# Reciprocals spread two slots later, transposes next to the masks, pair 1 split earlier, first weights converted step by step

## The chip, the cores and the metric

The kernel runs on one core of a Trainium2 chip. The time is in device microseconds for one execution, and less is better. Five engines work beside each other, each on its own queue in order: TensorE (PE in the profile, with PEld for its weight loads), VectorE (DVE), ScalarE (ACT), GpSimd (POOL) and SyncE (SP), which issues the transfers. Semaphores join the queues.

## The reference

Causal attention over 2 x 12 heads with 448 tokens of 64 channels, then two dense blocks on the 896 x 768 result:

```python
scores = q @ k.T / 8, masked above the diagonal; attn = exp(scores - max) / (sum + 1e-9)
x = attn @ v                                        # heads side by side: 896 x 768
x = (sigmoid(x @ w_gate) * (x @ w_val)) @ w_out     # 768 -> 1536 -> 768
h = x @ w_in; s = h * softmax(h)                    # 768 -> 1024
out = layer_norm(s) * g_ln @ w_out2                 # 1024 -> 768
```

## The kernel before

Every float32 operand is split into a high and a low part, and a product is three matmuls of parts. The attention takes the 24 heads as 12 pairs. The dense stages follow (lines L574, L604, L634, L695); there TensorE runs without a break.

The order of the attention is written out by hand. A loop counts slots `s`; a pair `p` owns the slots from `8 p` on, so that eight slots are one period. The table `STEPS` holds (offset, engine, step): a step of pair `p` is issued in slot `8 p + offset`. In a slot each engine goes through the table once, in the table's order, and takes the steps that are due; each engine's queue then keeps that order. What the slots of a steady period hold, with the names used below:

- Scores: `sc_mm(p, g)` puts the mask into a PSUM tile by matmuls with an identity (L329), then adds q k (L338). Group 0 holds the query blocks with 448 and 64 keys, group 1 those with 320 and 192.
- Maxima: `sc_max` on VectorE (L351), one instruction for both heads of a pair: max-448 in slot 0, max-64 in slot 1, max-320 in slot 4, max-192 in slot 5.
- Exponentials: `sc_exp` on ScalarE (L358), two instructions (one per head) for each maximum, one or so slots later: exp-448, exp-64, exp-320, exp-192. Each also leaves its row sum in `sum_t`, the tile that the maxima are written to as well. VectorE therefore waits for exp-448 before max-64, and for exp-320 before max-192.
- Sums and reciprocals: `sums` on GpSimd (L363) after exp-192, `recips` on VectorE (L367) in the next pair's slot 0, ahead of that pair's max-448. `rs_wide` (L221, rx) spreads the reciprocals on GpSimd, `rs_mm` (L381, r) transposes them on TensorE, `rs_out` (L219, rb) copies them out on ScalarE.
- Transposes of the exponentials: `tr_mm` (L409, t) on TensorE four times a pair, each followed by `tr_hi` on ScalarE (L416, pt) and `tr_lo` on VectorE (L229, pt).
- Values: `pv_mm` (L441, x) in eight pieces, then `x_mul` on VectorE (L447, xf), `x_hi` on ScalarE (L219, xy) and `x_lo` on GpSimd (L229, xy), some 21 to 23 slots after the pair's first slot.
- Operands of the next pair: `prep_k_hi`, `prep_q_hi` on GpSimd, `prep_k_lo` (L229, qks) and `prep_q_lo` (L249, qks) on VectorE. The values are split on GpSimd (`prep_v_hi`, `prep_v_lo`: L229, v).
- Weights of the first dense stage: `bits_steps` converts a chunk in four steps, one on ScalarE (L112) and three on VectorE (L115, L117, L120); `chunk_hi` (ScalarE, L131) and `chunk_lo` (VectorE, L134) split it. Chunks 0 to 3 are converted from slot 88 on. From slot 96 on two of 36 matmuls of the first dense tile (L473, gv) are issued in each slot.
- `keep_warm(24)` in slots 2, 5 and 9 are matmuls that nobody reads (L308).

Of the kernel before, what the change touches and what calls it, by code (L numbers as in the profile page):

```python
# [12 lines left out]
BF16 = mybir.dt.bfloat16  # L13
# [31 lines left out]
def attn_moe_moe2(ctx: ExitStack, tc: tile.TileContext, qk, v, w_gv, w_out, w_in2, w_out2, g_ln, out):  # L45
# [3 lines left out]
    nc = tc.nc  # L49
# [9 lines left out]
    ident = const.tile([128, 128], F32, name="ident")  # L59
    identx = const.tile([128, 128], F32, name="identx")  # L60
    identb = const.tile([128, 128], BF16, name="identb")
    maskb = const.tile([128, 128], BF16, name="maskb")
    g_sb = const.tile([128, NF2], F32, name="g_sb")
    mhalf = const.tile([128, 1], F32, name="mhalf")

# [124 lines left out]
    with ExitStack() as actx:  # L190
# [80 lines left out]
        for i in range(2):  # L271
# [47 lines left out]
        def sc_mm(p, g):  # L319
            both = ps_s.tile([128, 2, 512], F32, tag="s", name="s")  # L320
            t = qk_sp[p]
            flat = t.rearrange("p c s -> p (c s)")
            c0 = 0
            for i in GROUPS[g]:
                n = QE[i]
                w = min(n, 128)
                ps = ps_sc[p, i] = both[:, :, c0:c0 + n]
                for e in range(2):
                    nc.tensor.matmul(out=ps[:, e, n - w:], lhsT=identb, rhs=maskb[:, 128 - w:],  # L329
                                     start=(c0 == 0), stop=False, skip_group_check=True)  # L330
                c0 += n
# [170 lines left out]

        def steps(s, eng):
            for s0, e, f in STEPS:
                p, r = divmod(s - s0, PER)
                if e == eng and r == 0 and (1 if s0 < 0 else 0) <= p < NPR:
                    f(p)


        for s in range(PER * NPR + 26):  # L510
            if s in (2, 5, 9):
                keep_warm(24)
# [10 lines left out]
            for c in range(2 * NE + 2):
                e = s - 88 - 9 * c
                if e == 0:
                    bits_now = bits_steps(c)
                if e in (0, 2, 4, 6):
                    next(bits_now)
                if e == 7 and c < 2 * NE:
                    chunk_hi(c)  # L530
                if e == 8 and c < 2 * NE:
                    chunk_lo(c)
# [230 lines left out]
```

## Time and profile before

| what | value |
|---|---|
| median of 3 runs | 514.15 us (514.12 to 514.21) |
| the profiled execution | 514.3 us, of which the span from the first to the last instruction is 512.5 us |
| granted TensorE clock, mean | 0.997 |
| attention with the first pairs' start | 0 to about 112 us |
| mixed end of attention and first dense tile | 110.8 to 129.5 us |
| dense stages | 129.5 to 512.5 us |

The span is the time between the first and the last instruction that the profiler saw; 1.8 us of the execution lie around it. A period of the attention is read from one max-448 to the next. A row of the timeline gives start, duration, engine, line, operation and operands; in brackets stands how long the engine sat idle before it and what released it. A wait for several semaphores is put down to the one that came last by the profile, so a name in brackets can be wrong where that engine had long been done.

### The profile page before, as it was taken

The numbers are of one execution on the slowest core, as the hardware profiler recorded it, in microseconds if no ns is written. First come the engines' busy times: TensorE is split into PE (matmuls) and PEld (weight loads), VectorE is DVE, ScalarE is ACT, GpSimd is POOL, SyncE is SP. The second block draws the span as 40 slices with busy tenths as digits, with TensorE's granted clock in tenths as the row PEclk, the third lists the DMA queues.
The fourth block names the chain that finished last, engine by engine and source line by source line (L and its number), as shares of the span: only waits on it lengthen the run. The fifth ranks groups of instructions, "written<-read, shape, count | busy, mean of one in ns | idle before, by whom it ended". The sixth has DMA issues, their size and how long they took to land.

```text
span 512.5 us, 7699 instructions
## 1 busy us (share of the span) xinstructions
PE 501.2 (98%) x2980; PEld 457.1 (89%) x2980; DVE 335.9 (66%) x512; ACT 226.4 (44%) x481; POOL 118.0 (23%) x203
## 2 busy tenths in 40 slices
PE   8899999989999999999999999999999999999997
PEld 8888888878899999999999999999998888899997
DVE  4578787887655777887777766766753887841210
ACT  4677777784532454345434432343324242432211
POOL 3375757552000000000000000000050587710000
PEclk9899999999999999999999999999999999999999
DMA  5632323112333154355433532354440221000101
GB/s 150 184 92 77 92 79 93 42 49 76 125 123 99 66 165 164 125 163 161 137 116 125 182 123 68 139 165 164 133 176 1 86 100 62 0 32 33 61 32 61
DMA packets 13204, 52.79 MB, mean 103 GB/s; under 512 B 1776, under 2 KB 2288, under 8 KB 13168
## 3 DMA queue, kind: packets, MB, share of 16 engines
q1 hardware_dynamic: 13168, 52.31, 31.4%
q8 instruction: 23, 0.38, 0.3%
q14 instruction: 13, 0.11, 0.1%
HBM read 49.55 MB, written 2.75 MB: 102 GB/s over the span
## 4 chain that ended last, share of the span: by engine, by line
PE 81%; DVE 6%; ACT 6%; POOL 5%; issue 1%; POOLq 0%; ACTq 0%
PE gv L574 33%; PE pm L604 17%; PE po L695 12%; PE h L634 11%; ACT p L358 4%; DVE sum L351 4%; POOL v L229 2%; DVE qks L229 2%; PE gv L473 1%; PE warm L308 1%; POOL rx L221 1%; PE tp L677 1%; PE x L441 1%; PE s L338 1%; PE t L409 1%
## 5 line engine op out<-in xcount | busy, mean ns | idle before, releaser
L574 PE MATMUL gv<-xy,hl 128*128 128x448 f32 x828 | 168.1, 365 | 0.6 <-ACT pre L478 0.6
L574 PEld LDWEIGHTS gv<-xy,hl 128*128 128x128 f32 x828 | 155.5, 188 | 13.2 <-ACT pre L478 1.0
L604 PE MATMUL pm<-g,hl 128*128 128x448 f32 x432 | 87.7, 365 | 0.0
L604 PEld LDWEIGHTS pm<-g,hl 128*128 128x128 f32 x432 | 81.2, 188 | 6.4
L621 POOL TENSOR_SCALAR t<-t,g_sb 128x768 f32<-128x768 f32 x8 | 9.0, 1123 | 248.1 <-PE pm L604 248.1
L134 DVE TENSOR_TENSOR hl<-t,hl 128x768 fp32r<-128x768 f32 x36 | 35.1, 975 | 40.2 <-ACT hl L131 38.4
L695 PE MATMUL po<-wo,lt 128*128 128x384 f32 x336 | 60.7, 340 | 0.0
L634 PE MATMUL h<-wi,xy 128*128 128x512 f32 x252 | 59.2, 395 | 0.0
L695 PEld LDWEIGHTS po<-wo,lt 128*128 128x128 f32 x336 | 58.7, 188 | 0.2 <-POOL wo L626 0.2
L358 ACT ACTIVATE p<-s,sum 128x448 f32<-128x448 f32 (+3 forms) x96 | 45.0, 478 | 29.9 <-DVE sum L351 14.9
L634 PEld LDWEIGHTS h<-wi,xy 128*128 128x128 f32 x252 | 47.2, 188 | 11.4
L120 DVE SCALAR_TENSOR_TENSOR t<-raw,t 128x768 int32<-128x768 int32 (+1 forms) x56 | 53.0, 946 | 1.7
L117 DVE SCALAR_TENSOR_TENSOR t<-raw,t 128x768 int32<-128x768 int32 (+1 forms) x56 | 52.6, 939 | 1.8
L441 PE MATMUL x<-pt,v 128*128 128x320 f32 (+3 forms) x252 | 53.5, 327 | 0.0
L112 ACT ACTIVATE raw<-raw 128x768 f32<-128x768 f32 (+1 forms) x56 | 47.9, 866 | 10.3 <-DMA raw<-in_wo_dram 6.0
L351 DVE TENSOR_REDUCE sum<-s 128x2 f32<-128x128 f32 (+3 forms) x47 | 31.6, 672 | 15.2 <-ACT p L358 13.4
L441 PEld LDWEIGHTS x<-pt,v 128*128 128x128 f32 x252 | 38.1, 190 | 2.0
L229 DVE TENSOR_TENSOR pt<-t,pt 128x512 fp32r<-128x512 f32 (+1 forms) x48 | 31.9, 667 | 3.8 <-ACT pt L416 3.8
L115 DVE TENSOR_SCALAR t<-raw 128x768 int32<-128x768 int32 (+1 forms) x56 | 30.6, 547 | 4.9 <-ACT raw L112 4.9
L171 DVE TENSOR_TENSOR lt<-tp,lt 128x512 fp32r<-128x512 f32 x14 | 9.7, 690 | 36.4 <-ACT lt L170 36.4
L131 ACT CAST hl<-t 128x768 fp32r<-128x768 f32 x36 | 30.0, 832 | 4.6 <-PE pm L604 4.2
L179 ACT ACTIVATE wk<-gv 128x448 f32<-128x448 f32 x23 | 11.3, 542 | 43.1 <-PE gv L574 43.1
(90 smaller groups left out, 542.7 us busy)
## 6 DMA issues: line engine op xcount, KB each, us to landing
raw<-in_gv_dram SPq DMA_DIRECT2D x24, 768.0 KB, 4.4
raw<-in_wo_dram SPq DMA_DIRECT2D x20, 768.0 KB, 4.3
raw<-in_wi_dram SPq DMA_DIRECT2D x12, 512.0 KB, 3.5
qkr<-in_qk_dram SPq DMA_DIRECT2D x22, 224.0 KB, 3.5
vr<-in_v_dram SPq DMA_DIRECT2D x12, 256.0 KB, 2.6
out_dram<-o SPq DMA_DIRECT2D x6, 384.0 KB, 2.3
qkr<-in_qk_dram SPq DMA_DIRECT2D x4, 112.0 KB, 2.7
out_dram<-o SPq DMA_DIRECT2D x2, 192.0 KB, 1.8
```

The source lines that it names most:

```text
L112: nc.scalar.activation(out=w1.bitcast(F32), in_=w1.bitcast(F32), func=AF.Copy, scale=2.0 ** -112)
L117: nc.vector.scalar_tensor_tensor(out=tt, in0=w1, scalar=-2 ** 31, in1=tt, op0=ALU.bitwise_and, op1=ALU.bitwise_or)
L120: nc.vector.scalar_tensor_tensor(out=tt, in0=w0, scalar=29, in1=tt, op0=ALU.logical_shift_right, op1=ALU.bitwise_or)
L134: nc.vector.tensor_tensor(out=lo, in0=t_t.pop(it), in1=f32(hi), op=ALU.subtract)
L229: (nc.gpsimd if eng == 'P' else nc.vector).tensor_tensor(out=out, in0=a, in1=b, op=ALU.subtract)
L351: nc.vector.reduce_max(out=sum_t[p % 3][:, 8 + i:16:NQ], in_=ps, axis=AX.X, negate=True)
L358: nc.scalar.activation(out=p_t[(2 * p + e) % NPB][:, POFF[i]:POFF[i] + n], in_=ps[:, 1 - e], func=AF.Exp, bias=mx, scale=1.0, accum_out=sm)
L441: nc.tensor.matmul(out=ps[:, 128 * j:], lhsT=l, rhs=pt_t[h][:, c, u, c0:c0 + S - 128 * j], start=(chunk == 0 and n == 0), stop=(chunk == 7 ...
L574: nc.tensor.matmul(out=ps[i, b], lhsT=w[:, a, cs], rhs=xy[kk][:, x, b * S:(b + 1) * S], start=(kk == 0 and a == 0 and x == 0), stop=(kk == ...
L604: nc.tensor.matmul(out=ps[b], lhsT=w[:, a, cs], rhs=g_t[kk][:, x, b * S:(b + 1) * S], start=(kk == 0 and a == 0 and x == 0), stop=(kk == N ...
L634: nc.tensor.matmul(out=h[:, n * 512:(n + 1) * 512], lhsT=xy[kk][:, a, tk], rhs=wi[n * NK + kk][:, c], start=(kk == 0 and i == 0), stop=(kk ...
L695: nc.tensor.matmul(out=ps[n], lhsT=lts[k // 4][:, a, k % 4], rhs=wo[k][:, c, cs], start=(k == 0 and i == 0), stop=(k == NF2 - 1 and i == 2))
```

## The change

The spreading of the reciprocals is issued two slots later (`rs_mm` offset 10 to 12, `rs_out` 11 to 13). The transposes move one slot and stand ahead of the scores in the table, so that two of a pair's four groups come directly in front of the mask matmuls. The pieces of `pv_mm` move by one slot. The mask of 448 and 64 keys becomes one matmul of 192 columns for each head in place of two. `x_mul` moves to the end of the table, behind the maxima. Pair 1's operands are split in slots 0 and 1, ahead of the maxima there. The last `keep_warm` has 12 matmuls. Chunks 0 and 1 of the weights are converted with one step in each of the periods from slot 18 on; chunk 2 follows in slots 102 to 114, and chunk 3 in the dense stage.

```diff
-    maskb = const.tile([128, 128], BF16, name="maskb")
+    maskb = const.tile([128, 192], BF16, name="maskb")
-        nc.vector.tensor_copy(out=maskb, in_=mask0)
+        nc.vector.tensor_copy(out=maskb[:, :128], in_=mask0)
+        nc.vector.tensor_copy(out=maskb[:, 128:], in_=mask0[:, 64:])
...
+            for n, (lo, hi) in enumerate(((320, 512),) if g == 0 else ((192, 320), (384, 512))):
                 for e in range(2):
+                    nc.tensor.matmul(out=both[:, e, lo:hi], lhsT=identb, rhs=maskb[:, :hi - lo], ...)
...
-              for u, a, s0 in ((1, 0, 9), (1, 1, 11), (0, 0, 13), (0, 1, 15))
-              for d, eng, f in ((0, 'E', tr_mm), (1, 'A', tr_hi), (2, 'D', tr_lo))),
-            *((13 + n, 'E', lambda p, n=n: pv_mm(p, n)) for n in range(len(CHUNKS))),
+              for u, a, s0 in ((1, 0, 10), (1, 1, 12), (0, 0, 14), (0, 1, 16))
+              for d, eng, f in ((0, 'E', tr_mm), (0, 'A', tr_hi), (1, 'D', tr_lo))),
+            *((14 + n, 'E', lambda p, n=n: pv_mm(p, n)) for n in range(len(CHUNKS))),
...
+        for c in range(2 * NE):
+            it = bits_steps(c)
+            for k in range(4):
+                weights[PER * (2 + 4 * c + k) + 2] = lambda it=it: next(it)
+            weights[PER * (2 + 4 * c + 3) + 3] = lambda c=c: chunk_hi(c)
+            weights[PER * (2 + 4 * c + 3) + 6] = lambda c=c: chunk_lo(c)
...
+            if s == 1:
+                prep_k_lo(1)
+                prep_q_lo(1)
```

VectorE, one steady period of before, from max-320 to the next pair's max-448 (`sum` is a maximum, `pt` a low part of a transpose, `xf` is `x_mul`, `qks` the operands, `rs` the reciprocals):

```order
L351 TENSOR_REDUCE sum_143<-s 128x2
L229 TENSOR_TENSOR pt<-t,pt 128x512
L447 TENSOR_TENSOR xf<-x,rb 128x448
L351 TENSOR_REDUCE sum_143<-s 128x2
L249 SCALAR_TENSOR_TENSOR qks<-qkr,qks 128x448
L229 TENSOR_TENSOR pt<-t,pt 128x448
L367 RECIPROCAL rs<-rs 128x8
L351 TENSOR_REDUCE sum_144<-s 128x2
```

The same place in the change, from a conversion step behind max-64 (L117) on:

```order
L117 SCALAR_TENSOR_TENSOR t<-raw,t 128x768
L229 TENSOR_TENSOR pt<-t,pt 128x512
L229 TENSOR_TENSOR qks<-qkr,qks 128x448
L352 TENSOR_REDUCE sum_144<-s 128x2
L229 TENSOR_TENSOR pt<-t,pt 128x512
L352 TENSOR_REDUCE sum_144<-s 128x2
L448 TENSOR_TENSOR xf<-x,rb 128x448
L249 SCALAR_TENSOR_TENSOR qks<-qkr,qks 128x448
L229 TENSOR_TENSOR pt<-t,pt 128x448
L368 RECIPROCAL rs<-rs 128x8
L352 TENSOR_REDUCE sum_145<-s 128x2
```

`x_mul` stood in front of max-192 and now stands behind it, and a conversion step has come between max-64 and the low part that follows.

ScalarE, the same place, before and then in the change (`rb` is `rs_out`, `xy` is `x_hi`; 320 and 192 are the exponentials):

```order
L219 COPY rb<-r 128x448
L416 CAST pt<-t 128x512
L358 ACTIVATE p_147,sum_142<-s,sum_142 128x320
L358 ACTIVATE p_148,sum_142<-s,sum_142 128x320
L416 CAST pt<-t 128x448
L219 CAST xy_76<-xf 128x448
L358 ACTIVATE p_147,sum_142<-s,sum_142 128x192
L358 ACTIVATE p_148,sum_142<-s,sum_142 128x192
```

```order
L417 CAST pt<-t 128x512
L219 COPY rb<-r 128x448
L359 ACTIVATE p_148,sum_143<-s,sum_143 128x320
L359 ACTIVATE p_149,sum_143<-s,sum_143 128x320
L417 CAST pt<-t 128x448
L219 CAST xy_76<-xf 128x448
L359 ACTIVATE p_148,sum_143<-s,sum_143 128x192
L359 ACTIVATE p_149,sum_143<-s,sum_143 128x192
```

`rs_out` moved behind a transpose's high part; `x_hi` stands, as before, in front of exp-192.

TensorE, around the second mask of a period, before and then in the change (`r` is `rs_mm`, `x` the values, `t` a transpose):

```order
L441 MATMUL x<-pt,v_0_138 128x448 x3
L381 MATMUL r<-identx,rx 128x128
L381 MATMUL r<-ident,rx 128x128 x3
L409 MATMUL t<-identx,p_148 128x128
L409 MATMUL t<-ident,p_148 128x128 x4
L441 MATMUL x<-pt,v_0_138 128x448 x2
L329 LDWEIGHTS identb
```

```order
L442 MATMUL x<-pt,v_1_140 128x448 x3
L410 MATMUL t<-identx,p_147 128x128
L410 MATMUL t<-ident,p_147 128x128 x4
L382 MATMUL r<-identx,rx 128x128
L382 MATMUL r<-ident,rx 128x128 x3
L331 LDWEIGHTS identb
```

`rs_mm` moved behind the transpose group, and the two matmuls of the values that stood between that group and the mask now come after the scores; the mask follows `rs_mm` directly.

## Rows read from the trace of the kernel before

**Rows 1.** page, part 1: busy time and share of the span, by engine
```profile
PE 501.2 (98%) x2980; PEld 457.1 (89%) x2980; DVE 335.9 (66%) x512; ACT 226.4 (44%) x481; POOL 118.0 (23%) x203
```

**Rows 2.** windows: stretch, us, busy (instructions) of PE, PEld, DVE, ACT, POOL, clock, DMA
```profile
57.94:66.68 8.74, 8.59 (x78) 7.58 (x78) 7.20 (x13) 6.64 (x24) 5.69 (x10) 1.00 0.31 83
...
101.57:110.76 9.19, 8.46 (x76) 7.32 (x75) 7.40 (x14) 7.45 (x24) 4.61 (x8) 1.00 0.00 1
110.76:129.50 18.74, 16.26 (x98) 14.20 (x96) 15.34 (x19) 9.95 (x20) 6.77 (x8) 1.00 0.25 85
129.50:297.60 168.10, 168.09 (x829) 155.86 (x830) 121.50 (x169) 71.15 (x109) 0.00 (x0) 1.00 0.41 136
```

**Rows 3.** timeline, one period, PE weight loads: start us, us, operands [idle before <-releaser]
```profile
61.42 0.14 PEld L381 LDWEIGHTS r<-identx,rx 128*128 128x128 f32 x1 [0.53 <-POOL rx L221]
```

**Rows 4.** timeline, the same period, VectorE
```profile
59.71 1.04 DVE L351 TENSOR_REDUCE sum<-s 128x2 f32<-128x896 f32 x1
...
62.22 0.29 DVE L351 TENSOR_REDUCE sum<-s 128x2 f32<-128x128 f32 x1 [0.87 <-ACT p L358]
...
62.70 0.69 DVE L229 TENSOR_TENSOR pt<-t,pt 128x512 fp32r<-128x512 f32 x1 [0.18 <-ACT pt L416]
...
65.60 0.61 DVE L447 TENSOR_TENSOR xf<-x,rb 128x448 f32<-128x448 f32 x1
...
66.28 0.56 DVE L351 TENSOR_REDUCE sum<-s 128x2 f32<-128x384 f32 x1
...
66.76 0.62 DVE L249 SCALAR_TENSOR_TENSOR qks<-qkr,qks 128x448 fp32r<-128x448 f32 x1
...
68.33 0.20 DVE L367 RECIPROCAL rs<-rs 128x8 f32<-128x8 f32 x1 [0.42 <-POOL rs L363]
```

**Rows 5.** timeline, the same period, ScalarE
```profile
65.12 0.53 ACT L358 ACTIVATE p<-s,sum 128x320 f32<-128x320 f32 x1 [0.95 <-DVE sum L351]
...
66.05 0.20 ACT L358 ACTIVATION_READ_ACCUMULATOR p<-s,sum 128x1 f32 x1
...
66.14 0.53 ACT L416 CAST pt<-t 128x448 fp32r<-128x448 f32 x1
...
66.56 0.58 ACT L219 CAST xy<-xf 128x448 fp32r<-128x448 f32 x1
...
67.02 0.44 ACT L358 ACTIVATE p<-s,sum 128x192 f32<-128x192 f32 x1
```

**Rows 6.** timeline, the same period, GpSimd
```profile
61.86 1.42 POOL L229 TENSOR_TENSOR v<-vr,v 128x384 fp32r<-128x384 f32 x2
...
68.04 0.26 POOL L363 TENSOR_SCALAR rs<-sum 128x8 f32<-128x8 f32 x1 [2.80 <-ACT p L358]
```

**Rows 7.** timeline, weight conversion on VectorE and a GpSimd subtract, end of the attention
```profile
106.06 0.75 DVE L115 TENSOR_SCALAR t<-raw 128x768 int32<-128x768 int32 x1
...
108.65 0.95 DVE L117 SCALAR_TENSOR_TENSOR t<-raw,t 128x768 int32<-128x768 int32 x1
...
119.97 1.14 POOL L229 TENSOR_TENSOR xy<-xf,xy 128x448 fp32r<-128x448 f32 x1 [3.27 <-ACT xy L219]
120.00 1.93 DVE L120 SCALAR_TENSOR_TENSOR t<-raw,t 128x768 int32<-128x768 int32 x1
```

**Rows 8.** timeline, the first three pairs, VectorE and PE
```profile
10.78 0.61 DVE L229 TENSOR_TENSOR qks<-qkr,qks 128x448 fp32r<-128x448 f32 x1
...
14.47 0.61 PEld L338 LDWEIGHTS s<-qks 64*128 64x128 f32 x8 [2.11 <-DVE qks L249]
...
15.33 1.04 DVE L351 TENSOR_REDUCE sum<-s 128x2 f32<-128x896 f32 x1
...
25.05 1.06 DVE L351 TENSOR_REDUCE sum<-s 128x2 f32<-128x896 f32 x1
```

**Rows 9.** timeline, after the last pair's exponentials, PE weight loads
```profile
112.71 0.14 PEld L409 LDWEIGHTS t<-identx,p 128*128 128x128 f32 x1 [1.04 <-ACT p L358]
...
115.04 0.14 PEld L381 LDWEIGHTS r<-identx,rx 128*128 128x128 f32 x1 [0.93 <-POOL rx L221]
```

More of the change, by code (lines that the diff above doesn't have):

```diff
@@ L324, in sc_mm @@
             for i in GROUPS[g]:
-                n = QE[i]
-                w = min(n, 128)
-                ps = ps_sc[p, i] = both[:, :, c0:c0 + n]
+                ps_sc[p, i] = both[:, :, c0:c0 + QE[i]]
+                c0 += QE[i]
+            for n, (lo, hi) in enumerate(((320, 512),) if g == 0 else ((192, 320), (384, 512))):
                 for e in range(2):
-                    nc.tensor.matmul(out=ps[:, e, n - w:], lhsT=identb, rhs=maskb[:, 128 - w:],
-                                     start=(c0 == 0), stop=False, skip_group_check=True)
-                c0 += n
+                    nc.tensor.matmul(out=both[:, e, lo:hi], lhsT=identb, rhs=maskb[:, :hi - lo],
+                                     start=(n == 0), stop=False, skip_group_check=True)
             for i in GROUPS[g]:
@@ L486, in attn_moe_moe2 @@
         STEPS = (
+            *((s0 + d, eng, lambda p, f=f, u=u, a=a: f(2 * p + a, u))
+              for u, a, s0 in ((1, 0, 10), (1, 1, 12), (0, 0, 14), (0, 1, 16))
+              for d, eng, f in ((0, 'E', tr_mm), (0, 'A', tr_hi), (1, 'D', tr_lo))),
+            (12, 'E', rs_mm),
             (0, 'E', lambda p: sc_mm(p, 0)), (4, 'E', lambda p: sc_mm(p, 1)),
-            *((s0 + d, eng, lambda p, f=f, u=u, a=a: f(2 * p + a, u))
-              for u, a, s0 in ((1, 0, 9), (1, 1, 11), (0, 0, 13), (0, 1, 15))
-              for d, eng, f in ((0, 'E', tr_mm), (1, 'A', tr_hi), (2, 'D', tr_lo))),
-            *((13 + n, 'E', lambda p, n=n: pv_mm(p, n)) for n in range(len(CHUNKS))),
-            (10, 'E', rs_mm),
+            *((14 + n, 'E', lambda p, n=n: pv_mm(p, n)) for n in range(len(CHUNKS))),
             (-7, ENG['kh'], prep_k_hi), (-6, ENG['qh'], prep_q_hi), (-5, ENG['kl'], prep_k_lo), (-2, 'D', prep_q_lo),
             (3, ENG['lk'], last_keys), (7, ENG['vh'], prep_v_hi), (9, ENG['vl'], prep_v_lo),
-            (7, 'P', sums), (8, 'D', recips), (8, ENG['rx'], rs_wide), (11, ENG['rr'], rs_out),
-            (21, 'D', x_mul), (22, ENG['xh'], x_hi), (23, ENG['xl'], x_lo),
+            (7, 'P', sums), (8, 'D', recips), (8, ENG['rx'], rs_wide), (13, ENG['rr'], rs_out),
+            (22, ENG['xh'], x_hi), (23, ENG['xl'], x_lo),
             (1, 'A', lambda p: sc_exp(p, 3)), (2, 'A', lambda p: sc_exp(p, 0)),
@@ L500, in attn_moe_moe2 @@
             (4, 'D', lambda p: sc_max(p, 2)), (5, 'D', lambda p: sc_max(p, 1)),
+            (21, 'D', x_mul),
         )
+        weights = {}
+        for c in range(2 * NE):
[4 more added lines that the diff above has]
+            weights[PER * (2 + 4 * c + 3) + 6] = lambda c=c: chunk_lo(c)
+        two = bits_steps(2 * NE)
+        for k in range(4):
+            weights[PER * NPR + 6 + 4 * k] = lambda: next(two)
         def steps(s, eng):
@@ L505, in steps @@
                 p, r = divmod(s - s0, PER)
-                if e == eng and r == 0 and (1 if s0 < 0 else 0) <= p < NPR:
+                if e == eng and r == 0 and (2 if s0 < 0 else 0) <= p < NPR:
                     f(p)
@@ L511, in attn_moe_moe2 @@
             if s in (2, 5, 9):
-                keep_warm(24)
+                keep_warm(24 if s < 9 else 12)
             steps(s, 'E')
@@ L517, in attn_moe_moe2 @@
             steps(s, 'A')
+            if s == 1:
+                prep_k_lo(1)
+                prep_q_lo(1)
             steps(s, 'D')
             steps(s, 'P')
+            if s == 0:
+                prep_k_hi(1)
+                prep_q_hi(1)
             if s in (8, 12):
                 dma_next()
[L523 to L532, printed above, removed]
+            if s in weights:
+                weights[s]()
         while left:
```

## Prediction

> **What bounds the kernel now.** The page's busy times come first [rows 1]. TensorE is busy for 98% of the span, and a reader might stop there. The windows by stage say more [rows 2]. From 129.50 us on TensorE works without a gap (168.09 of 168.10 us), so a microsecond that the attention loses or gains moves the end by a microsecond. In a steady attention period TensorE shows 8.59 of 8.74 us, but matmuls overlap in that figure; its weight loads fill 7.58 us. The timeline of one period then shows that TensorE even waits 0.53 us for the spread reciprocals [rows 3].
>
> What sets the 8.74 us is a ring through VectorE, ScalarE and GpSimd. To be seen in the timeline: max-448 starts at 59.71; max-64 waits 0.87 us for exp-448 and starts at 62.22; a transpose's low part (pt) follows at 62.70 after 0.18 us for its high part; behind it on VectorE stand the key's low part and max-320 [rows 4]. Exp-320 waits 0.95 us for that maximum and starts at 65.12; its second sum is read by 66.25; pt, `x_hi` (66.56) and exp-192 (67.02) follow without a gap [rows 5]. `sums` waits for exp-192 and starts at 68.04 [rows 6], the reciprocals wait for `sums` (68.33) [rows 4], and the next max-448 stands behind them in VectorE's queue. Every step starts when the one before it ends. A step put into this ring costs its whole time; one removed elsewhere gains nothing.
>
> **The change, part by part.** *`x_mul` behind max-192.* Before, `x_mul` runs at 65.60, while exp-320 is under way, and `x_hi` finds it done. Max-192 starts at 66.28, 0.03 us after exp-320's second sum: it waits for it [rows 4, 5]. In the change `x_mul` cannot start before max-192 has gone. What follows max-192 on VectorE starts 0.48 us after it (66.28 to 66.76), so `x_mul` starts at 66.76, takes 0.61 us to 67.37, and `x_hi` starts at about 67.40. Exp-192 still stands behind `x_hi` on ScalarE and starts 0.46 us after it (66.56 to 67.02), so at 67.86 and not at 67.02. That is 0.84 us in the ring, 9.58 us a period. It holds in every pair that has an older pair's `x_mul` in front of its exp-192: pairs 2 to 11, ten times, **+8.4 us**. Bounds: 0.75 if the handovers are shorter, 0.90 if max-192's whole 0.56 us passes first.
>
> *Conversion steps in the attention.* Per chunk L115, L117 and L120 each come once behind max-64, where only 0.18 us are free [rows 4]. L117 took 0.95 us [rows 7]; with the overlap that successive VectorE instructions show, it pushes the rest of the ring by at least 0.6 us, and L115 by 0.4. That is the cost if nothing slows them. But GpSimd splits the values from 61.86 to 63.28 at that place [rows 6], and L120 beside a GpSimd subtract took 1.93 us, ending 0.82 us after it [rows 7]. By that row a step here would end at 64.10, and the low part would start 1.4 us late; L115 0.9. I take the middle, 1.1, 1.1 and 0.7, since the split is two instructions and the first ends earlier. `chunk_lo` comes where VectorE has 0.42 us free before the reciprocals [rows 4] and costs 0 to 0.25, taken as 0.1. The two ScalarE steps lie in the 0.95 us in which it waits for max-320 [rows 5], at no cost; without that cover up to 0.9 each. Together 3.0 a chunk, **+6.0 us** for two, between 3.2 and 7.9.
>
> The Trainium skill (SBUF — State Buffer, Who interferes with whom) says that a VectorE instruction with two inputs in SBUF and a GpSimd instruction that reads SBUF take a shared port pair in turn, and the later one blocks until the other is through. The 1.93 us row agrees with that; by the rule alone the steps would cost near 7.9, without it 3.2.
>
> *The spread two slots later, and the transposes at the masks.* TensorE loses its 0.53 us wait [rows 3] and two mask matmuls a pair. Nothing in the ring waits for TensorE at that place, so it then waits elsewhere: **0**. `rs_out` moves within ScalarE's 0.95 us wait: 0. Its result is wanted by an `x_mul` a period later. On GpSimd's and SP's queues nothing changes place in a steady period but the weights' transfers, which go out earlier.
>
> *Pair 1 split ahead of the maxima.* The key's low part (0.61 us at 10.78) leaves the way of max-320 of pair 0, and the scores of pair 1 no longer wait (TensorE idles 2.11 us before 14.47) [rows 8]. Pair 1's max-448 then comes some 0.5 us earlier. Its ring took 9.72 us (15.33 to 25.05), against 8.74 later; with TensorE no longer behind, and 12 matmuls fewer in front of it, I take 8.5: **-1.7 us** in all, between 1.0 and 2.1.
>
> *End of the attention.* Pair 11's period, 9.19 us [rows 2], held conversion steps that are gone: **-0.5 us**. Then TensorE idled 1.04 us until pair 11's first transpose and 0.93 us for rx [rows 9], both behind VectorE's conversions; and 4 of the 36 matmuls of the first dense tile (0.20 us each by 168.09 / 829) [rows 2] can go before pair 11's exponentials are done. At most 2.8, at least 1.2, taken **-2.2 us**: one of the two waits may be followed by another. Chunk 3 is converted in the dense stage, where VectorE is busy 121.50 of 168.10 us [rows 2]: 0, at worst its three instructions' 2.9.
>
> Sum: 8.4 + 6.0 - 1.7 - 0.5 - 2.2 = +10.0 us. The profiled execution took 514.3 us, 512.5 of it span; the median is 514.15, 0.15 below. On the median: **524.2 us**. All low ends: 7.5 + 3.2 - 2.1 - 0.5 - 2.8 = +5.3 (519.5); all high ends: 9.0 + 7.9 - 1.0 - 0.4 - 1.2 = +14.3 (528.5).
>
> **Rivals.** *TensorE sets the pace, and the change is faster.* For it: 8.59 of 8.74 us busy [rows 2], with a wait of 0.53 us that ends. If the ring had slack, ten periods would gain 0.53 us each, the conversions would hide, and the start and end gains would come on top: -5.3 - 1.7 - 0.5 - 2.2 = -9.7, 504.5 us. It decides if exp-192 can start by about 67.0 in spite of `x_mul`. Against it: VectorE, ScalarE and GpSimd wait for each other all round the period, and exp-192 stands behind `x_hi` in one queue.
>
> *The conversions hide.* If the longer ring leaves VectorE room elsewhere that they can use, 6.0 falls away: 518.2 us. Against it: they stand in front of pt and max-320 in a queue that has 0.18 us free there.
>
> *The gains and the losses cancel.* It would need a ring longer by no more than 0.4 us and hidden conversions: 514.2 us. Nothing in the rows speaks for it.
>
> **How the numbers follow.** Forecast 0.82, conversions hidden 0.08, TensorE sets the pace 0.07, cancel 0.03. About 0.2%, 1 us, is what a measurement of this kernel can tell from no change. So slower 0.90, same 0.03, faster 0.07. The forecast's own ends are 519.5 and 528.5; taking in the second rival, the range is 518.0 to 528.5, which leaves out the two other rivals and a little of the forecast's tails.
>
> **What would show it.** Right: periods of 9.5 to 9.6 us where no conversion falls and 10 to 11 us where L117 or L120 does; `x_hi` preceded by a ScalarE wait for `xf`; no TensorE wait for rx; pair 2's max-448 near 23.3 us; the first L574 near 139 us. Wrong: periods at or under 8.7 us, `x_mul` done before exp-320 ends, conversion steps of 0.95 us that delay nothing, or a granted clock below 1.00 in the steady periods, which is 1.00 now [rows 2] and is in none of the sums.

## The result

The changed kernel takes **520.1 us** (median of 4 runs, 519.12 to 520.27), the kernel before 514.18 us on the same chip: a ratio of 1.0108, 95% interval 1.009 to 1.0125. The change makes the kernel 1.1% slower, by 5.9 us; forecast were 10.0 us. The profiled execution took 519.97 us, 518.2 us of it span (before: 514.3 and 512.5).

For the experiments below: the 1260 matmuls of the first two dense stages run at one of two paces, 203 or 207 ns from one start to the next at the same granted clock, which is 5.0 us of the time, and three kernels change between the two from one execution to the next; the traces of before and after are both at 203.

The profile page of after, busy time by engine, beside [rows 1]:

```profile
PE 502.1 (97%) x2944; PEld 455.1 (88%) x2944; DVE 333.5 (64%) x513; ACT 226.9 (44%) x481; POOL 120.0 (23%) x203
```

All engines are as busy as before to within 3 us, so this view does not show where 5.7 us of span went. The windows do. They go from one max-448 to the next, to the end of pair 11's exp-192, to the first matmul of the dense stage, and through that stage (stretch, us, busy time and instructions of PE, PEld, DVE, ACT, POOL, clock, DMA share, GB/s), beside [rows 2]:

```profile
62.86:72.31 9.45, 8.75 (x76) 7.54 (x75) 7.08 (x14) 7.52 (x23) 5.65 (x11) 1.00 0.28 76
82.14:92.37 10.23, 9.03 (x76) 7.62 (x76) 8.05 (x15) 6.73 (x22) 6.43 (x11) 1.00 0.26 72
92.37:102.65 10.28, 9.20 (x76) 7.71 (x76) 8.81 (x16) 7.57 (x23) 6.48 (x11) 1.00 0.41 145
112.10:120.80 8.70, 8.43 (x70) 7.63 (x70) 5.66 (x10) 6.26 (x22) 4.06 (x7) 1.00 0.00 1
120.80:135.54 14.74, 13.84 (x85) 12.48 (x83) 7.24 (x11) 6.06 (x12) 5.79 (x8) 1.00 0.00 1
135.54:303.60 168.06, 168.06 (x829) 155.79 (x830) 121.94 (x170) 71.16 (x109) 0.00 (x0) 1.00 0.41 135
```

A steady period that holds no VectorE step of the conversion is 9.45 us where it was 8.74. With L117 it is 10.23, with L120 and `chunk_lo` 10.28. The dense stage starts at 135.54 us in place of 129.50 and is as long as before. The loss is in the periods.

One period of after on VectorE (start us, duration us, engine, line, operation, operands, in brackets the idle time before it and what ended it), beside [rows 4]:

```profile
62.86 1.04 DVE L352 TENSOR_REDUCE sum<-s 128x2 f32<-128x896 f32 x1
...
65.36 0.29 DVE L352 TENSOR_REDUCE sum<-s 128x2 f32<-128x128 f32 x1 [0.87 <-ACT p L359]
65.84 0.69 DVE L229 TENSOR_TENSOR pt<-t,pt 128x512 fp32r<-128x512 f32 x1 [0.18 <-ACT pt L417]
66.45 0.94 DVE L229 TENSOR_TENSOR qks<-qkr,qks 128x448 fp32r<-128x448 f32 x1
67.31 0.81 DVE L352 TENSOR_REDUCE sum<-s 128x2 f32<-128x640 f32 x1
...
69.32 0.56 DVE L352 TENSOR_REDUCE sum<-s 128x2 f32<-128x384 f32 x1 [0.60 <-ACT p L359]
69.79 0.62 DVE L448 TENSOR_TENSOR xf<-x,rb 128x448 f32<-128x448 f32 x1
...
72.19 0.20 DVE L368 RECIPROCAL rs<-rs 128x8 f32<-128x8 f32 x1 [0.71 <-POOL rs L364]
```

And the same period on ScalarE, beside [rows 5]:

```profile
68.16 0.53 ACT L359 ACTIVATE p<-s,sum 128x320 f32<-128x320 f32 x1
...
69.17 0.53 ACT L417 CAST pt<-t 128x448 fp32r<-128x448 f32 x1
70.44 0.56 ACT L219 CAST xy<-xf 128x448 fp32r<-128x448 f32 x1 [0.73 <-DVE xf L448]
70.91 0.41 ACT L359 ACTIVATE p<-s,sum 128x192 f32<-128x192 f32 x1
```

This is the new wait. Max-192 waits 0.60 us for exp-320, as it had to before; that wait was filled with `x_mul` and is now empty. `x_mul` runs behind max-192, `x_hi` waits 0.73 us for it, and exp-192, ready to go since max-192, stands in the queue behind `x_hi`. VectorE gains nothing by it: beside those 0.60 us, its wait for the sums is longer too (0.71 us for 0.42).

TensorE no longer waits for the spread reciprocals [rows 3]; it waits for the query's low part, which now stands behind `x_mul` (its weight loads in the same period):

```profile
70.99 0.61 PEld L339 LDWEIGHTS s<-qks 64*128 64x128 f32 x8 [0.76 <-DVE qks L249]
```

The conversion of chunk 0 on VectorE, beside [rows 7], and GpSimd's split of the values with the query's high part behind it (L234), first beside L117, then in a period without a VectorE step. The split is two instructions, which [rows 6] shows as one row; here they are taken one by one:

```profile
35.25 0.87 DVE L115 TENSOR_SCALAR t<-raw 128x768 int32<-128x768 int32 x1
45.08 1.26 DVE L117 SCALAR_TENSOR_TENSOR t<-raw,t 128x768 int32<-128x768 int32 x1
...
46.86 0.80 DVE L229 TENSOR_TENSOR qks<-qkr,qks 128x448 fp32r<-128x448 f32 x1
47.58 0.81 DVE L352 TENSOR_REDUCE sum<-s 128x2 f32<-128x640 f32 x1
...
55.30 1.26 DVE L120 SCALAR_TENSOR_TENSOR t<-raw,t 128x768 int32<-128x768 int32 x1
```

```profile
44.52 1.00 POOL L229 TENSOR_TENSOR v<-vr,v 128x384 fp32r<-128x384 f32 x1
45.48 1.17 POOL L229 TENSOR_TENSOR v<-vr,v 128x128 fp32r<-128x128 f32 x1
46.62 0.56 POOL L234 TENSOR_SCALAR qks<-qkr 128x448 fp32r<-128x448 f32 x1
...
65.92 0.46 POOL L229 TENSOR_TENSOR v<-vr,v 128x128 fp32r<-128x128 f32 x1
66.35 0.57 POOL L234 TENSOR_SCALAR qks<-qkr 128x448 fp32r<-128x448 f32 x1
```

The start, beside [rows 8], max-448 of pairs 1 and 2:

```profile
15.14 1.04 DVE L352 TENSOR_REDUCE sum<-s 128x2 f32<-128x896 f32 x1
23.22 1.04 DVE L352 TENSOR_REDUCE sum<-s 128x2 f32<-128x896 f32 x1
```

From these rows the balance is made, after against before. Up to pair 2's max-448: 23.22 - 25.05 = -1.83 us. From there to pair 11's max-448: 88.88 - 78.29 = +10.59, which is nine times 0.73 and, for the three kinds of conversion period, twice 0.38, 0.78 and 0.83, to within 0.05 us. Pair 11 to the end of exp-192: 8.70 - 8.80 = -0.10. From there to the dense stage: 14.74 - 17.36 = -2.62. Together +6.04 us at the start of the dense stages; the last 0.34 us to the +5.7 of the span are gained behind it.

### The profile page after: what moved, and what is told of

Same layout as the page of the kernel before. It is cut to its first block, busy times and chain, and to the rows that moved or that the text cites. A ratio compares the mean times of both kernels' runs of the same rounds, so it can differ in the third digit from the quotient of the medians.

```text
span 518.2 us, 7607 instructions
## 1 busy us (share of the span) xinstructions
PE 502.1 (97%) x2944; PEld 455.1 (88%) x2944; DVE 333.5 (64%) x513; ACT 226.9 (44%) x481; POOL 120.0 (23%) x203
## 4 chain that ended last, share of the span: by engine, by line
PE 78%; ACT 8%; DVE 7%; POOL 3%; issue 3%; POOLq 0%; DVEq 0%; ACTq 0%
PE gv L584 32%; PE pm L614 17%; PE h L644 11%; PE po L705 11%; ACT p L359 6%; DVE sum L352 3%; PE gv L474 2%; POOL xy L229 1%; PE x L442 1%; PE tp L687 1%; PE warm L309 1%; DVE qks L229 1%; ACT xy L219 1%; DVE xf L448 1%; DVE pt L229 1%
## 5 line engine op out<-in xcount | busy, mean ns | idle before, releaser
L584 PE MATMUL gv<-xy,hl 128*128 128x448 f32 x828 | 168.1, 365 | 0.6 <-ACT pre L479 0.6
L705 PE MATMUL po<-wo,lt 128*128 128x384 f32 x336 | 60.0, 338 | 0.0
L644 PE MATMUL h<-wi,xy 128*128 128x512 f32 x252 | 59.4, 397 | 0.0
L705 PEld LDWEIGHTS po<-wo,lt 128*128 128x128 f32 x336 | 58.2, 188 | 0.1
L644 PEld LDWEIGHTS h<-wi,xy 128*128 128x128 f32 x252 | 47.4, 188 | 11.4
L117 DVE SCALAR_TENSOR_TENSOR t<-raw,t 128x768 int32<-128x768 int32 (+1 forms) x56 | 53.2, 950 | 1.8
L120 DVE SCALAR_TENSOR_TENSOR t<-raw,t 128x768 int32<-128x768 int32 (+1 forms) x56 | 52.6, 940 | 1.7
L442 PE MATMUL x<-pt,v 128*128 128x320 f32 (+3 forms) x252 | 49.0, 322 | 0.3
L339 PE MATMUL s<-qks 64*128 64x448 f32 (+3 forms) x288 | 28.5, 319 | 5.1 <-DVE qks L249 5.1
L115 DVE TENSOR_SCALAR t<-raw 128x768 int32<-128x768 int32 (+1 forms) x56 | 30.7, 549 | 2.8 <-ACT raw L112 2.8
```

The lines of the kernel that those rows point to most:

```text
L117: nc.vector.scalar_tensor_tensor(out=tt, in0=w1, scalar=-2 ** 31, in1=tt, op0=ALU.bitwise_and, op1=ALU.bitwise_or)
L120: nc.vector.scalar_tensor_tensor(out=tt, in0=w0, scalar=29, in1=tt, op0=ALU.logical_shift_right, op1=ALU.bitwise_or)
L442: nc.tensor.matmul(out=ps[:, 128 * j:], lhsT=l, rhs=pt_t[h][:, c, u, c0:c0 + S - 128 * j], start=(chunk == 0 and n == 0), stop=(chunk == 7 ...
L584: nc.tensor.matmul(out=ps[i, b], lhsT=w[:, a, cs], rhs=xy[kk][:, x, b * S:(b + 1) * S], start=(kk == 0 and a == 0 and x == 0), stop=(kk == ...
L644: nc.tensor.matmul(out=h[:, n * 512:(n + 1) * 512], lhsT=xy[kk][:, a, tk], rhs=wi[n * NK + kk][:, c], start=(kk == 0 and i == 0), stop=(kk ...
L705: nc.tensor.matmul(out=ps[n], lhsT=lts[k // 4][:, a, k % 4], rhs=wo[k][:, c, cs], start=(k == 0 and i == 0), stop=(k == NF2 - 1 and i == 2))
```

## The experiments

Each is the changed kernel or the kernel before with a few lines altered. Times are medians, ratios are against the kernel before on the same chip. "Dense start" is the start of the first matmul of L574 (129.50 us before, 135.54 us after).

### `x_mul` back in front of the maxima, in the changed kernel

```diff
+            (21, 'D', x_mul),
             (0, 'D', lambda p: sc_max(p, 3)), ...
-            (21, 'D', x_mul),
```

> The changed kernel with x_mul back in front of the maxima, all else as in the change. Ring theory: exp-192 no longer waits for x_mul; periods without a conversion go from 9.45 back to 8.7 us, ten of them give 7.3 us, so 512.8 us. Rival (the longer periods come from the moved transposes, values or reciprocals): the periods stay at 9.4 and the time at 520.

Measured: 517.43 us (517.26 to 518.42), ratio 1.0065 (1.005 to 1.008). The attention did what the ring demands: periods without a VectorE conversion step fell to 8.4 to 8.5 us, and the dense start came to 128.97 us, 6.57 us earlier than after. The total did not follow, because of the dense stages. The groups of TensorE instructions by line, of this kernel (line, engine, operation, operands, count, then busy us and mean ns of one):

```profile
L584 PE MATMUL gv<-xy,hl 128*128 128x448 f32 x828 | 171.4, 368 | 0.6 <-ACT pre L479 0.6
L614 PE MATMUL pm<-g,hl 128*128 128x448 f32 x432 | 89.4, 368 | 0.0
```

and of the changed kernel:

```profile
L584 PE MATMUL gv<-xy,hl 128*128 128x448 f32 x828 | 168.1, 365 | 0.6 <-ACT pre L479 0.6
L614 PE MATMUL pm<-g,hl 128*128 128x448 f32 x432 | 87.7, 365 | 0.0
```

171.4 / 828 is 207 ns, 168.1 / 828 is 203 ns; 3.3 + 1.7 = 5.0 us. Less these, the time is 512.4 us, near the 512.8 expected. The granted clock is 1.00 in both, and the count and shape of the matmuls are the same.

### Only `x_mul` behind the maxima, in the kernel before

```diff
-            (21, 'D', x_mul), (22, ENG['xh'], x_hi), ...
+            (22, ENG['xh'], x_hi), ...
...
+            (21, 'D', x_mul),
         )
```

> The kernel before with nothing but x_mul moved behind the maxima. Ring theory: periods of 9.45 in place of 8.74 us for pairs 2 to 11, so 514.2 + 7.1 = 521.3 us. Rival (TensorE sets the pace and VectorE's order has slack): 514.2 us.

Measured: 522.1 us (521.53 to 522.79), ratio 1.0152 (1.0137 to 1.0167). The periods are 9.55 to 9.58 us, the dense start 137.97 us. VectorE and ScalarE of one period:

```profile
70.09 0.56 DVE L351 TENSOR_REDUCE sum<-s 128x2 f32<-128x384 f32 x1 [0.60 <-ACT p L358]
```

```profile
71.22 0.57 ACT L219 CAST xy<-xf 128x448 fp32r<-128x448 f32 x1 [0.73 <-DVE xf L447]
71.69 0.41 ACT L358 ACTIVATE p<-s,sum 128x192 f32<-128x192 f32 x1
```

This one line of the table costs 8 us by itself, more than the whole change (the periods from pair 2 to pair 11 are 7.55 us longer, pair 11 to the end of exp-192 0.47); the price of 0.84 us a period was right for before's order.

### Only the spread two slots later, in the kernel before

```diff
-            (10, 'E', rs_mm),
+            (12, 'E', rs_mm),
...
-            (11, ENG['rr'], rs_out),
+            (12, ENG['rr'], rs_out),
```

> The kernel before with the spread of the reciprocals alone moved: rs_mm from offset 10 to 12, in front of the scores, rs_out from 11 to 12. Ring theory: the wait of 0.53 us for rx goes away on TensorE and another takes its place; 514.2 us. Rival (TensorE sets the pace): ten periods shorter by up to 0.53 us, 508.9 us.

`rs_mm` also moves to the head of the table, ahead of the scores.

Measured: 514.5 us (513.78 to 515.32), ratio 1.0004 (0.9994 to 1.0013), periods 8.77 us. TensorE's wait for the reciprocals is gone and nothing is gained; the same stretch now holds an idle 0.57 us in front of a transpose. The rival by which TensorE sets the pace (508.9 us) falls.

### The conversion at its old place, in the changed kernel

```diff
-            if s in weights:
-                weights[s]()
+            for c in range(2 * NE + 2):
+                e = s - 88 - 9 * c
...
```

> The changed kernel with chunks 0 to 3 converted from slot 88 on as before. Ring theory: 4.0 us of conversion steps (0.4, 0.8 and 0.8 twice) leave the periods, and some 3.0 us come back in pair 11's period and behind it, so 519.1 us. Rival (the steps hide in the ring): only the 3.0 us come, 523.1 us.

Measured: 519.75 us (519.43 to 520.0), ratio 1.0107 (1.009 to 1.0124), periods 9.51 us, dense start 134.98 us. From pair 2's to pair 11's max-448 it is 85.36 us for 88.88: the steps' 4.0 us are gone, but the plain periods are 9.51 in place of 9.45, so 3.5 us are left. From there to the dense stage it is 26.25 us for 23.44, 2.8 us given back. Where the first weights are converted is worth some 0.4 us in the time, within the spread of the runs, and 0.7 in these stretches.

### `x_hi` behind exp-192, in the changed kernel

```diff
-            (22, ENG['xh'], x_hi), (23, ENG['xl'], x_lo),
+            (23, ENG['xl'], x_lo),
...
             (5, 'A', lambda p: sc_exp(p, 2)), (6, 'A', lambda p: sc_exp(p, 1)),
+            (22, ENG['xh'], x_hi),
```

> The changed kernel, with x_mul left behind max-192 as the change has it, and x_hi moved from in front of exp-192 to behind it on ScalarE. Theory (the ring of waits): max-192, x_mul, x_hi, exp-192 stand in one chain, and what the change lost in a period is that exp-192 waits for x_mul through x_hi. With x_hi behind, exp-192 waits for max-192 alone: the 0.73 us of the wait go, and the 0.46 us of x_hi's slot with them at the most. Period without a conversion step 8.3 to 8.7 us in place of 9.45; ten periods give 510 to 513 us, or up to 5 us more if the dense stage runs at the 207 ns a matmul that the kernel with x_mul in front showed. Rival (VectorE's load): x_mul costs a period its 0.6 us wherever it stands behind the maxima, because the maxima of the next pair come later: period 9.45, time 520. Not faster than 519 would show that x_hi is not the link.

Measured: 514.23 us (513.69 to 515.06), ratio 1.0002 (0.9992 to 1.0011), at 203 ns a dense matmul. `x_mul` is still behind max-192, and 5.5 us are back by the ratios (5.9 by the medians, which are of two chips): what the change lost was not VectorE's time but that exp-192 stood behind `x_hi`. ScalarE, and VectorE at the end of the period:

```profile
66.72 0.42 ACT L359 ACTIVATE p<-s,sum 128x192 f32<-128x192 f32 x1 [0.20 <-DVE sum L352]
```

```profile
68.56 1.09 DVE L352 TENSOR_REDUCE sum<-s 128x2 f32<-128x896 f32 x1 [0.18 <-PE s L339]
```

Exp-192 now waits for its maximum alone. The period fell to 8.76 us, just above what was expected, and the total lies 1.2 us above its range: max-448 waits for the scores here, which wait for the query's low part behind `x_mul`. With the ring opened, TensorE's chain is next.

### Only the start, in the kernel before

```diff
-                if e == eng and r == 0 and (1 if s0 < 0 else 0) <= p < NPR:
+                if e == eng and r == 0 and (2 if s0 < 0 else 0) <= p < NPR:
...
+            if s == 1:
+                prep_k_lo(1)
+                prep_q_lo(1)
             steps(s, 'D')
```

and likewise `prep_k_hi(1)`, `prep_q_hi(1)` in slot 0, and 12 matmuls in the last `keep_warm`.

> The kernel before with only the start of the change: the split of pair 1 ahead of the maxima of pair 0, in two slots of its own, and half of the filler matmuls later on. Theory: max-448 of pair 2 comes 1.7 to 1.9 us earlier (23.2 to 23.4 us in place of 25.05), the ten periods stay at 8.73 us, and the end keeps it: 512.4 us (512.1 to 512.9). Rival: the gain is given back, because the first periods wait for something later (the keys of pair 2, or the transposes): 514.2 us, with a longer period behind pair 2.

Measured: 513.02 us (median of nine runs from 512.17 to 513.38; the profiled execution took 1251.03 us and is left out, so no period is known), ratio 0.9975 (0.9965 to 0.9985). That is a gain of 1.3 us by the ratio, at the small end of the expectation. But all nine runs show a mean granted clock of 1.00, and of the 29 runs of the kernel before that they are held against only seven do (median 513.81 us; the others show 0.997 and 514.54). Against those seven the start is worth 0.8 us. What the clock has to do with it stands further below, with the start's term.

### `x_mul` in front, and the conversion at its old place

The changed kernel with the edits of the first and the fourth experiment.

> The changed kernel with x_mul in front of the maxima again and the conversion steps from slot 88 on, as before. Theory: with x_mul in front, VectorE has no long idle stretch in a period, so each conversion step adds to it (0.5, 0.9 and 1.25 us in the run with x_mul in front alone), 5.3 us in all; taken out, the ten periods are 8.4 to 8.5 us, the tail is 2.5 us longer as in the kernel before, and the dense stage begins near 126.0 us, 3 us earlier: 514.4 us if the dense matmuls stand at 207 ns, 509.6 us if at 203 ns. Rival: the place of the conversion is a wash here as it was with x_mul behind (0.35 us): 517.1 us, or 512.3 us at 203 ns.

Measured: 516.32 us; nine runs between 515.81 and 517.2 us and one of 510.85. Here one and the same program shows both paces of the dense matmuls. The profiled run had 207 ns, and the time is near the rival's. The periods were 8.70 us in a row and the dense start 127.71 us, not 8.4 to 8.5 and 126.0: a short period in the first experiment was one that followed the start or a period lengthened by a conversion. What is left of the change in this kernel, the spread, the transposes, the masks and the start, moves the period from 8.73 to 8.70 us and the dense start by the start's 1.8 us.

### `x_mul` in front and `x_hi` behind exp-192

The changed kernel with the edits of the first and the fifth experiment.

> The changed kernel with x_mul in front of the maxima and x_hi behind exp-192. Theory: in the run with x_mul in front, exp-192 starts 0.46 us behind max-192's end only because x_hi stands in front of it; with x_hi behind, the period is 8.0 to 8.3 us in place of 8.45, and the time is 2 to 4 us below that run: 513.4 to 515.4 us at 207 ns a dense matmul, 508.6 to 510.6 us at 203 ns. Rival (the ring is bounded elsewhere, by the transposes' evictions on VectorE): period 8.45, time 517.4 us, or 512.6 us at 203 ns. On the pace of the dense matmuls: theory, it is set by how that stage is entered and flips with the order of the work ahead of it; rival, it goes with x_mul's place in front, and is 207 ns here too.

Measured: **512.45 us** (511.92 to 513.25), ratio 0.9968 (0.9958 to 0.9977), at 203 ns. Dense start 127.94 us; the period without a VectorE step is 8.26 to 8.33 us, near the theory, but the total is the rival's. Faster than both kernels. The rival on the dense pace falls, since `x_mul` is in front here too. The gain over the first experiment's attention is 1.0 us, not 2 to 4: with less slack in the period the same conversion steps cost more (0.64, 1.04 and 1.55 us).

### The same, with the conversion at its old place

> x_mul in front of the maxima, x_hi behind exp-192, and the conversion steps from slot 88 on. Theory: in the run with x_mul in front and x_hi behind, the six steps and the low parts of chunks 0 and 1 lengthen their periods by 0.64, 1.04 and 1.55 us, 6.5 us in two chunks; taken out of the periods and put behind them they cost the tail some 2.5 to 3.4 us. The ten periods at 8.3 us, the dense stage near 124.5 us, 508.4 to 509.5 us at 203 ns a dense matmul (513.5 to 514.5 at 207 ns). Rival: the plain period of 8.3 us that this order showed was short only because a conversion stood in the period ahead of it, as with x_mul in front alone (8.4 to 8.5 us between conversions, 8.70 us in a row without); then 8.5 to 8.6 us in a row, and 511 to 512 us.

Measured: **511.15 us** (508.89 to 515.14), ratio 0.9934 (0.991 to 0.9959), the fastest of all. Periods alternate between 8.27 and 8.58 us (mean 8.41), between theory and rival; the dense start is 125.67 us in the profiled run, which was the one of 515.14 us with all dense matmuls at 207 ns. Of the others four took 508.9 to 509.0 us, at a mean granted clock of 0.999 to 1.00, and five 511.15 to 511.64 us, all at 0.996. So the median stands for the second group; at full clock and 203 ns the kernel takes 509.0 us. In which stage the clock fell no trace shows, since only the 207 ns execution was profiled.

### Conversion steps right behind max-448, with `x_mul` in front and `x_hi` behind

```diff
-                weights[PER * (2 + 4 * c + k) + 2] = lambda it=it: next(it)
+                weights[PER * (2 + 4 * c + k)] = lambda it=it: next(it)
```

> x_mul in front, x_hi behind exp-192, and each conversion step two slots earlier, right behind max-448, where VectorE then waits 0.88 us for exp-448 once a period. Theory (a step costs what is left when the wait that it fills is used up): the row for L115 at 0.55 us and those for L117 and L120 at 0.95 us alone fit the wait nearly whole, and the periods grow by 0 to 0.5 us in place of 0.64, 1.04 and 1.55: 508 to 509.5 us at 203 ns a dense matmul. Rival (the step delays pt's low part, which stands behind it and for which TensorE waits): no gain, 512.4 us.

Measured: 516.19 us; nine runs from 515.72 to 516.75 us, and 510.62 us in the profiled one, whose dense matmuls stood at 203 ns. Against the same kernel without this edit the dense start is 1.8 us earlier, of which 0.5 us is the start of pair 2. The conversion periods are 0.58, 0.93 and 1.38 us longer than a plain one, in place of 0.64, 1.04 and 1.55. The wait of 0.88 us that the step was to fill is hardly used; the next experiment shows the reason in the changed kernel's order.

### The same edit in the changed kernel itself

> The changed kernel as it is, with each conversion step two slots earlier, right behind max-448. It asks what the conversions cost in the change's own order, where the prediction said 6.0 us and the periods show 4.0. Theory (filled waits): here VectorE waits 0.60 us in front of max-64 for exp-448, so L115 costs nothing and L117 and L120 0.2 to 0.5 us each: 517.5 to 518.7 us. Rival (VectorE's sum of work counts, not the place): unchanged at 520.1 us.

Measured: 524.05 us (523.84 to 524.36), ratio 1.0195 (1.0178 to 1.0212), with 171.4 and 89.4 us for the two dense groups, that is at 207 ns; 519.1 us less the 5.0. The dense start is 134.74 us, 0.8 us earlier than after. The conversion periods are longer than a plain one by 0.20, 0.61 and 0.66 us. TensorE, VectorE and GpSimd in the one with L117:

```profile
45.05 0.30 PE L410 MATMUL t<-identx,p 128*128 128x128 f32 x1 [1.13 <-DVE pt L229]
```

```profile
43.36 0.95 DVE L117 SCALAR_TENSOR_TENSOR t<-raw,t 128x768 int32<-128x768 int32 x1
44.23 0.68 DVE L229 TENSOR_TENSOR pt<-t,pt 128x512 fp32r<-128x512 f32 x1
44.91 0.29 DVE L352 TENSOR_REDUCE sum<-s 128x2 f32<-128x128 f32 x1
...
47.44 0.82 DVE L352 TENSOR_REDUCE sum<-s 128x2 f32<-128x640 f32 x1 [0.68 <-PE s L339]
```

```profile
43.46 1.33 POOL L221 TENSOR_SCALAR rx<-rs 128x512 f32<-128x512 f32 x1
```

The wait in front of max-64 is 0.87 us in after (0.60 is the one in front of max-192), so the theory had even more room than it counted on. The step does fill that wait (max-64 follows with none). But it delays the low part of the transpose behind it, TensorE waits 1.13 us for that (0.27 in after), its scores come 0.9 us later in the period, and max-320 waits 0.68 us for them. rx on GpSimd takes twice as long beside it (0.62 us undisturbed). A wait on one engine was free only for work that nobody else is waiting behind.

### The low part of v moved away from the conversion step

```diff
-            (9, ENG['vl'], prep_v_lo),
+            (11, ENG['vl'], prep_v_lo),
```

> The changed kernel with one row of the table altered: the low part of v, GpSimd's 1.42 us, two slots later, so that it no longer runs beside the conversion step. It asks how much of a step's price is the two engines holding each other up. Theory (contention): L115, L117 and L120 take 0.87, 1.26 and 1.26 us beside v's low part and 0.55, 0.95 and 0.95 us where nothing stands beside them, and the longer periods shrink by about 0.3 us each, 1.8 us in six: 518.3 us, with 1.4 us for v's low part everywhere in place of 2.13. Rival: whatever GpSimd does in v's place (the keys' and queries' high parts) holds VectorE up as much, or the wait is elsewhere: 520.1 us.

Measured: 525.2 us (524.68 to 525.78), ratio 1.0218 (1.0203 to 1.0233), at 207 ns; 520.2 less the 5.0. The dense start is 135.99 us, 0.45 us later than after. VectorE and GpSimd in the period with L117, to be held against the rows of after above:

```profile
45.19 0.95 DVE L117 SCALAR_TENSOR_TENSOR t<-raw,t 128x768 int32<-128x768 int32 x1
46.05 0.68 DVE L229 TENSOR_TENSOR pt<-t,pt 128x512 fp32r<-128x512 f32 x1
46.66 1.16 DVE L229 TENSOR_TENSOR qks<-qkr,qks 128x448 fp32r<-128x448 f32 x1
47.74 0.81 DVE L352 TENSOR_REDUCE sum<-s 128x2 f32<-128x640 f32 x1
```

```profile
46.32 1.81 POOL L229 TENSOR_TENSOR v<-vr,v 128x384 fp32r<-128x384 f32 x2
```

L117 takes 0.95 us as expected, 0.31 less. But the key's low part, now beside v, takes 1.16 us in place of 0.80. From max-64 to max-320 it is 2.76 us here and 2.71 us in after. The conversion periods are longer than a plain one by 0.37, 0.77 and 0.83 us, as in after to 0.01 us. So the theory falls, and the rival's time came: the two engines hold each other up as much as before, at another place. In after the step loses 0.31 us beside v, and the key's low part, at 0.80 for the 0.94 of a plain period, is spared 0.14; here the step loses nothing, and the key's low part starts while v's first instruction is under way.

## Why the prediction was right, and where its sizes were off

**The mechanism was right.** The ring through max-192, `x_mul`, `x_hi` and exp-192 is what the change lengthened. Of what was to show it, the wait of `x_hi` for `xf` is there (0.73 us), TensorE's wait for rx is gone, and the period is 9.45 us (9.5 to 9.6). From max-192 to exp-192 it is 1.59 us (69.32 to 70.91) in place of 0.74, the forecast's 0.84 to within 0.01. Pair 2's max-448 comes at 23.22 us (23.3 was said), but not for the reason given, as told below. Undoing this one line takes 6.57 us off the attention; doing it alone costs 8 us; taking `x_hi` out of exp-192's way returns 5.5 us with `x_mul` left where it is. The dense start, near 139 us in the forecast and 135.54 measured, is off.

**The ring's term, 8.4 us forecast, 7.0 measured.** It was counted ten times at 0.84 us. Nine periods cost 0.73, and pair 11, which has no next pair's operands to prepare, is 0.45 longer to the end of exp-192 than a plain period of before (8.70 us for 8.25); the second experiment has 0.47 there (9.27 for 8.80, both with conversion steps). In before's order the price is 0.84, as said. Of the 0.11 us between, about half goes with the other reorderings (9.51 us a period with the conversion moved away, against 9.57). The rows place it between the key's low part and max-320: 0.86 us from start to start in after, and 0.96 in this row of before and the next:

```profile
63.30 0.98 DVE L229 TENSOR_TENSOR qks<-qkr,qks 128x448 fp32r<-128x448 f32 x1
64.26 0.83 DVE L351 TENSOR_REDUCE sum<-s 128x2 f32<-128x640 f32 x1
```

Which of the moved instructions brings it was not separated.

**The conversion's term, 6.0 us forecast, 4.0 measured.** This is the mis-sized step. The prediction took 0.7, 1.1 and 1.1 us, halfway to an L120 of 1.93 us beside GpSimd, plus 0.1 for `chunk_lo`. Measured are 0.38, 0.78 and 0.83 (the last with `chunk_lo`), and the rows give the sum. Undisturbed, the next VectorE instruction starts 0.87 us after L117 and 0.47 after L115, as in the last two experiments. Of this 0.27 us were free before, between max-64 and the low part. That leaves 0.60 and 0.20. Beside GpSimd a step loses 0.31 us (L117 takes 1.26 for 0.95), and the key's low part behind it is spared 0.14 (0.80 for 0.94). Together they make 0.77 and 0.37. So the contention is real, but its net price was 0.17 us a step, where the forecast charged 0.3 to 0.5.

The Trainium skill (SBUF — State Buffer, Who interferes with whom) has the later of the two engines blocked until the other is through. Taken one by one, the instructions agree with it nearly to the full. In after v's first instruction has 0.44 us left when L117 starts, and L117 loses 0.31; L117 has 0.86 left when v's second starts, and that loses 0.71 (1.17 for 0.46). The key's low part loses 0.33 of 0.47 to L234 in the plain period (0.94 for the 0.61 of [rows 8]) and, coming later behind a step, 0.19 of 0.32. In the eleventh experiment rx loses 0.71 of the 0.85 that L117 had left; in the twelfth the key's low part loses 0.55 of 0.67 to v's first instruction; in [rows 7] L120 lost 0.98 of 1.11. Each loses what the earlier one had left, less 0.12 to 0.15 us. A small copy of 64 x 64 on GpSimd beside L117 in the twelfth experiment lost less, 0.47 of 0.86 (0.96 for 0.49). The 7.9 us that the prediction drew from the rule let a step wait for the whole split, by a row with a single GpSimd instruction; in the rows of after a step waits only for what is left of the split's first instruction.

**Start, pair 11 and the end.** The start was forecast at -1.7 and came to -1.83, but that it fits is luck. The prediction took pair 1's 9.72 us [rows 8] for TensorE being behind. In the profiled execution of before, the granted clock fell there: 0.90 from 14 to 16 us, 0.50 (the lower level, 1.2 GHz) from 16 to 18 and 0.75 from 18 to 20, and 1.00 on either side. This is the window of the start and its 24 filler matmuls, then the same matmuls and max-448 of pairs 1 and 2 in the third experiment, which has the old start and 1.00 there:

```profile
6.80:22.60 15.80, 13.80 (x159) 12.68 (x157) 7.90 (x14) 8.22 (x30) 6.81 (x14) 0.89 0.63 188
15.12 2.09 PEld L308 LDWEIGHTS <-identb 128*128 128x128 bf16 x24
```

```profile
15.79 1.34 PEld L308 LDWEIGHTS <-identb 128*128 128x128 bf16 x24
16.00 1.04 DVE L351 TENSOR_REDUCE sum<-s 128x2 f32<-128x896 f32 x1
24.08 1.05 DVE L351 TENSOR_REDUCE sum<-s 128x2 f32<-128x896 f32 x1
```

At full clock pair 1 takes 8.08 us with the old start as with the new one; in the second experiment, where the clock fell as in before, it takes 9.73. So 1.6 us of the 1.83 belong to the clock of one execution and 0.2 to pair 1's earlier max-448, where 0.5 was said. Pair 2's max-448 itself stands anywhere from 22.57 to 23.95 us in the ten profiles with the new start. At equal clock the sixth experiment has the start at 0.8 us, and the change as a whole then costs some 6.4 us (an estimate: 520.1 less the 513.6 to 513.8 of before's runs at 1.00). Whether the new start keeps the clock up is not shown: TensorE idled 2.11 us ahead of the fall [rows 8], but 2.09 us in the third experiment too, where the clock stayed.

Pair 11 lost the conversion steps of before, 0.55 us (8.80 against 8.25) where 0.5 was said; the 9.19 us that the prediction read for it are of a window that begins 1.77 us ahead of its max-448. The end of the attention gave 2.6 us for 2.2.

**The dense stages, forecast 0, gave 0.35 us.** Two groups differ: L705 takes 60.0 us and L695 before it 60.7, L644 59.4 and L634 59.2. All profiles with the changed order show the new pair (60.0 or 60.1), all with the old order (before, second and third experiment) the old one. So neither `x_mul`'s place nor the spread does it; which edit does was not asked.

The new sum: 7.0 + 4.0 - 1.8 - 0.55 - 2.6 - 0.35 = +5.7 us, the measured difference of the spans.

**The rivals.** That TensorE sets the pace is refuted by the spread alone (514.5 us). That the conversions hide is not what happens in the periods; but moving them early costs, with what the end gives back, only 0.4 us, so the time fell between this rival's 518.2 us and the forecast. The prediction had counted the early steps and the shorter end as two terms, +6.0 and -2.2 with -0.5; together they came to +0.8 in the sum above.

## What to carry to other kernels

In a loop whose period is a ring of waits, an instruction is free while it runs in a wait of its engine that it does not lengthen, and costs its whole time where it stands between a wait's end and the instruction that others wait for; look for the instruction in front of it in the queue (here `x_hi` in front of exp-192) before moving anything else. A free slot on one engine is only free if nobody waits for what stands behind it. Contention is to be charged by the one instruction that is under way when the other starts, not by the whole group, and what stands behind may be spared a part of it. And before a gain at one place is booked, the granted clock of that place is to be read.

## What the runs showed of the hardware

Two paces of the same matmuls at the same clock. The 828 and 432 matmuls of 448 columns in the first two dense stages stand 203 ns apart on average in some executions and 207 ns in others, from the first of them to the last, at a granted clock of 1.00, with the same count and shapes. All 4 runs of after and all 10 each of the fifth and the eighth experiment fit 203; all 4 each of the first, the eleventh and the twelfth fit 207; the seventh, the ninth and the tenth kernels gave both (510.85 against 515.8 to 517.2 us, 515.14 against 508.9 to 511.6, and 510.62 against 515.7 to 516.8). So it is settled for each execution, and the odds go with the order of the attention ahead of it. What sets it stays open: neither the time at which the stage is entered (203 at 126.17, 127.94, 129.21 and 135.54 us; 207 at 125.67, 127.71, 128.97 and 134.74 us) nor anything else read here tells the two apart. An effect of 5 us that flips by itself is as large as the change that was studied; the windows of the attention, not the total, settled most of these experiments.
